# Most K and V loads of a decode block issued by GpSimd as software DMAs instead of by SyncE

## The chip, the cores and the metric

The kernel runs on one core of one Trainium2 chip. Time is device time of one execution in microseconds. The engines are named as in the profile: PE (TensorE, matrix multiplication; PEld are its weight loads), DVE (VectorE), ACT (ScalarE), POOL (GpSimd) and SP (SyncE, which computes nothing and here issues loads). Sixteen DMA engines move the data between the chip's memory and the core's on-chip memory of 128 partitions.

## The reference

One decode step of a transformer block in float32, for two sequences with one new token each. Attention over a cache of 8192 keys, 32 heads of 128, then a residual sum and an MLP (512 to 1792 to 512) with its own layer norms:

```
q = layernorm(x) @ wq                              # 2 x 512 by 512 x 4096
scores = einsum("bhqd,bhkd->bhqk", q, k_cache) * 128 ** -0.5
p = softmax(scores)                                # over 8192 keys
h = x + einsum("bhqk,bhkd->bhqd", p, v_cache) @ wo
y = layernorm(layernorm(h))
out = h + gelu(y @ w1 + b1) @ w2 + b2
```

The caches are 268 MB each, of the 561 MB that the kernel reads. Each number of them is used once.

## The kernel before

**Units and slots.** The work on the caches is cut into 32 units, numbered 0 to 31: unit 2g + b is the pair of heads 2g, 2g + 1 of sequence b. Its K tile and its V tile are 8 MB each: 64 KB in each of 128 partitions (128 rows of 128 numbers). Three slots of this size hold them: K tiles go to slots 0 and 1 in turn, V tiles to slot 2, only the last V tile to slot 1. At the end slot 0 takes wo, and then the weights of the MLP. Text below calls the tiles K0 to K31 and V0 to V31.

**A K tile** is multiplied by q in place by DVE in two chunks (L441), the first of 80 rows and the second of 48. POOL adds the two halves of each row of the first chunk (L445, the halving), DVE sums up the second chunk and then the halved first one (L449), and takes the largest score (L456). Unit 0 has four chunks of 32 and three halvings. After the second unit of a pair, the exponentials (L473, ACT) are made for both.

**A V tile** is used as the moving side of 32 products on PE, in float32 two passes each (L236, or L188 where the code isn't in the loop), two units later: in iteration i the kernel multiplies V of unit i - 2.

**The order of issue.** Each engine works through its own list in the order in which the code is written; waits are set by a helper (class Waits) that follows who wrote and read which part of a tile. One iteration i of the loop writes, in this order: the load of V(i-2) (V0 comes in iteration 1, V1 in iteration 3), the load of K(i+1), the multiplications and the halving of unit i, the products with V(i-2), the sums of unit i. A load waits until the last reader of what its slot held is done: for V that is PE, with the products on the V tile before, for K it is DVE, with the sums of the unit two before it.

**The start.** SP issues wq (8 MB, to slot 2), K0 in two halves and K1 at once; V0 waits for the products with wq.

**The end.** load_wo writes, after the loop, the load of wo by SP into slot 0 and a gather of 64 rows of wog (0.5 MB) by POOL, which is the only software DMA of the kernel. Then follow V30, the projection by wo (project_all), the products with V30, V31 in two parts of 96 and 32 rows of each partition's 128, a memset by POOL for the biases (L590), and the loads of the biases, w1 (L594) and w2 (L598). [...]

**Semaphores.** K and V loads count on one semaphore for each of K and V and each b (waits.own); the other DMAs take 16 in turn for hardware and 16 for software.

Of the kernel before, what the change touches and what calls it, by code (L numbers as in the profile page):

```python
# [16 lines left out]
SHORT = (32, 32, 32, 32)  # L17
NG = 4
TH = 2
FILL = (24, 1, 4, 2, 3)  # L20
SR = 4
LW = 6
# [13 lines left out]
class Waits:  # L36
# [76 lines left out]
    def place(self, eng, op, areas):  # L113
        areas = [(x, w) for x, w in areas if x is not None]
        queue = (eng,)
        if "DMA" in op:
            kind = "soft" if eng == "Pool" else "hard"
            proc = kind, self.lane.get(kind, 0) % self.LANES
            if kind == "hard" and self.own:
                proc = self.own  # L120
            else:
                self.lane[kind] = self.lane.get(kind, 0) + 1
        else:
            proc = queue
        self.sem(proc)
        need = {}
        if proc != queue and self.count[proc]:
            need[proc] = self.count[proc]
        for (name, parts, cols), writes in areas:
            for r in self.mem.get(name, ()):  # L130
                if not (writes or r[4]) or not (r[2] & parts and r[3] & cols):
                    continue
                if r[0] == proc == queue:
                    if eng == "PE" or eng != "Pool" and not r[4]:
                        continue
                need[r[0]] = max(need.get(r[0], 0), r[1])
        clock = self.clock.setdefault(queue, {})
        todo = []
        for p, t in sorted(need.items(), key=lambda x: -self.after[x[0], x[1]][0]):
            if clock.get(p, 0) >= t:  # L140
                continue
            todo.append((p, t))
            for q, u in self.after[p, t][1].items():
                clock[q] = max(clock.get(q, 0), u)
        tick = self.count[proc] + 1
        if op != "Ldweights":
            self.count[proc] = tick
            self.after[proc, tick] = (len(self.after), {**clock, proc: tick})
        for (name, parts, cols), writes in areas:
            held = self.mem.setdefault(name, [])  # L150
            if writes:
                held[:] = [r for r in held if r[2] & ~parts or r[3] & ~cols]
            else:
                held[:] = [r for r in held if r[4] or r[0] != proc or r[2] & ~parts or r[3] & ~cols]
            held.append((proc, tick, parts, cols, writes))
        return proc, todo[::-1]
# [108 lines left out]
def tile_decode_block(nc, waits, x, k, v, wq, wo, wog, w1, bias, w2, out):  # L265
    B, H, SK, DH = k.shape
# [23 lines left out]
    def slot(at):  # L290
        return kv.tile([P, ROW], F32, name="kv", tag="kv", at=at)
# [22 lines left out]
    nc.gpsimd.memset(lt4, 0.0)  # L314
    oall = const.tile([P, H - TH, B], F32, name="oall")
    og = const.tile([P, SR, B], F32, name="og")
# [90 lines left out]
    def load(src, i, parts):  # L407
        g, b = units[i]
        t = slot(i % 2 if src is k or i == NU - 1 else 2)
        rows = src[b, 2 * g:2 * g + 2].rearrange("h (p j) d -> (h p) (j d)", j=NS2)  # L410
        waits.own = ("v" if src is v else "k", b) if len(parts) == 1 else None
        for s0, n in parts:
            nc.sync.dma_start(t[:, s0 * DH:(s0 + n) * DH], rows[:, s0 * DH:(s0 + n) * DH])
        waits.own = None
        return t

# [68 lines left out]
    def values(i, t):  # L485
        g, b = units[i]
        so, nu, w = so2[g == GL], NS2 // 4, 16
        for u in range(nu):
            n = u % NG
            if i == NU - 1 and u == 0:  # L490
                keep_warm(FILL[0])
            pe.matmul(so[32 * n:32 * n + w], ptz[b][:, u, :], t[:, u * 512:(u + 1) * 512],
# [26 lines left out]
    def project_all(wot):  # L519
        so = so2[0]  # L520
        parts = [(oall[:, h, :], wot[:, h, :]) for h in range(GA)]
        parts += [(og[:, r, :], wgt[:, r, :]) for r in range(SR)]
        parts += [(oall[:, h, :], wot[:, h - 2, :]) for h in range(GA + 2, H - TH)]
        n = len(parts)
# [7 lines left out]
    full = [(0, NS2)]  # L532
    assert NS2 == sum(LONG) == sum(SHORT)
    KT, VT = {0: load(k, 0, [(0, NS2 // 2), (NS2 // 2, NS2 // 2)])}, {}
    for i, (g, b) in enumerate(units):
        if i == 1 or i >= 3:
            j = max(i - 2, 0)
            VT[j] = load(v, j, full)
        if i + 1 < NU:
            KT[i + 1] = load(k, i + 1, full)  # L540
# [64 lines left out]
    def cut(parts, n):  # L605
        at[0] += n
        return late[:parts, at[0] - n:at[0]]

    zeros = cut(P, (TH + 1) * 32)
    nc.gpsimd.memset(zeros, 0.0)  # L610
    otz = zeros[:, :TH * 32].rearrange("p (s m) -> p s m", s=TH)
    lane = zeros[:B, TH * 32:]
    nc.gpsimd.tensor_copy(lane[:, 0:B], ident[:B, :B])
# [4 lines left out]

    wl = wot[:, H - 2 - TH:, :]
    wsum = const.tile([P, TH], F32, name="wsum")  # L620
# [20 lines left out]
    def keep_warm(n):  # L641
        for _ in range(n):
            pe.matmul(wp, wb[:, :P], wb, start=True, stop=True)
# [9 lines left out]
    def spread(row):  # L653
        return row.rearrange("d (n j c) -> d n c j", n=NG, c=DC)
# [8 lines left out]
    nc.vector.tensor_copy(b1t, b1p)  # L663
    keep_warm(FILL[1])
    for s in range(TH):
        for n in range(NG):
            pe.matmul(pc[32 * n:32 * n + 32], otz[:, s], spread(wlc[:, s])[:, n], start=False, stop=(s == TH - 1))
    keep_warm(FILL[2])
    cen = cut(P, DC * 32)
# [11 lines left out]
    for s in range(TH):  # L681
        for n in range(NG):
            pe.matmul(po2[32 * n:32 * n + 32], otz[:, s], wl[:, s, n * P:(n + 1) * P], start=False, stop=False)
    keep_warm(FILL[3])
    FH = FN // 2
# [10 lines left out]
    nc.scalar.activation(junk[:, 1:2], std, AF.Gelu_apprx_tanh)  # L696
    keep_warm(FILL[4])

# [67 lines left out]
```

## Time and profile before

| | |
|---|---|
| median of 3 runs | 1303.33 us (1303.16 to 1303.37) |
| profiled execution | 1303.13 us, of which the span of the program is 1301.3 us |
| busy | DVE 973.6 us (75%), PE 385.9 (30%), POOL 364.6 (28%), ACT 49.1 (4%) |
| DMA | 561.13 MB, 431 GB/s over the span; hardware queue 560.48 MB, software queue 0.52 MB |
| chain that ended last | 57% DMA, 37% DVE |

The chain is followed back from the last instruction to what released each step; a wait for a load counts from the load's issue, so that part of a load's time in it is time in the queue behind other loads. Share of 16 engines, in the table of queues, is the time that the packets of a queue took, of what 16 engines have in the span or in the stretch asked for; it can pass 100% in a short stretch, since packets are counted where they start. One packet is one piece of contiguous memory: 64 KB for a K or V tile's partition. Time to landing is from the start of the issuing instruction until the load's semaphore is full.

### The profile page before, as it was taken

What the parts mean: (1) busy time and instruction counts of PE and PEld (TensorE: products, weight loads), DVE (VectorE), ACT (ScalarE), POOL (GpSimd) and SP (SyncE); (2) the same over time, 40 slices, a digit from 0 to 9 for tenths busy, and PEclk for the clock granted to TensorE, in tenths of its full rate; (3) what the DMA queues carried; (4) which work ended last, traced back from release to release, by engine and by line L of the source; (5) the groups of instructions that cost most, each with busy time, mean ns of one, the idle gap of its engine ahead of it and who ended that gap; (6) DMA issues with size and microseconds to landing.
All of it is one profiled execution on the core that took longest, in us unless ns stands there. A gap on an engine that the chain in (4) does not pass through costs nothing.

```text
span 1301.3 us, 6275 instructions
## 1 busy us (share of the span) xinstructions
PE 385.9 (30%) x2756; PEld 118.2 (9%) x2756; DVE 973.6 (75%) x284; ACT 49.1 (4%) x156; POOL 364.6 (28%) x64
## 2 busy tenths in 40 slices
PE   3002322213332122333203232212323212332369
PEld 0000100101010010101001010000101001010113
DVE  1989989777779777779877778877778977777911
ACT  0000000000000000000000000000000000000011
POOL 1433333311333321233321233331133331133300
PEclk9556665566666556666556666556666556666569
DMA  9999999999999999999999999999999999999998
GB/s 403 435 451 420 447 421 445 425 429 439 423 447 423 445 422 447 423 437 433 425 443 425 443 423 447 421 441 429 433 437 423 445 423 447 421 445 425 438 422 373
DMA packets 10821, 561.13 MB, mean 431 GB/s; under 512 B 1398, under 2 KB 1398, under 8 KB 1660
## 3 DMA queue, kind: packets, MB, share of 16 engines
q1 hardware_dynamic: 10664, 560.48, 99.6%
q0 software_dynamic: 144, 0.52, 0.1%
q8 instruction: 5, 0.08, 0.0%
q14 instruction: 4, 0.03, 0.0%
q10 hardware_dynamic: 4, 0.00, 0.0%
HBM read 561.53 MB, written 0.00 MB: 432 GB/s over the span
## 4 chain that ended last, share of the span: by engine, by line
DMA 57%; DVE 37%; issue 2%; POOL 2%; PE 1%; SPq 0%; POOLq 0%
DMA kv<-in_k_dram 50%; DVE kv L441 22%; DVE s L449 15%; DMA kv<-in_w_dram 3%; POOL kv L445 2%; DMA wgt<-in_wog_dram,gidx 2%; DMA kv<-in_wq_dram 2%; PE so L188 1%; DVE qs L395 0%; DVE oall L507 0%; PE qps L188 0%; DVE rl L482 0%; PE sm L236 0%; SPq L598 0%; DVE q L385 0%
## 5 line engine op out<-in xcount | busy, mean ns | idle before, releaser
L441 DVE TENSOR_TENSOR kv<-kv,qps 128x10240 f32<-128x10240 f32 (+1 forms) x66 | 554.5, 8423 | 206.3 <-DMA kv<-in_k_dram 205.8
L445 POOL TENSOR_TENSOR kv<-kv 128x5120 f32<-128x5120 f32 (+1 forms) x34 | 356.0, 10470 | 864.8 <-DVE kv L441 864.8
L236 PE MATMUL so<-kv,pt 128*16 128x512 f32 x1920 | 273.6, 734 | 708.4 <-DMA kv<-in_v_dram 708.4
L449 DVE TENSOR_REDUCE s<-kv 128x48 f32<-128x6144 f32 (+1 forms) x66 | 381.5, 5820 | 1.4 <-POOL kv L445 0.3
L236 PEld LDWEIGHTS so<-kv,pt 128*16 128x16 f32 x1920 | 57.6, 113 | 901.1 <-DMA kv<-in_v_dram 712.6
L497 ACT ACTIVATE ss<-so 128x512 f32<-128x512 f32 x16 | 9.6, 597 | 1062.1 <-PE so L236 1047.8
L473 ACT ACTIVATE pt<-s,nb 64x128 f32<-64x128 f32 x64 | 25.5, 399 | 141.8 <-DVE nb L468 140.5
L236 PE MATMUL sm<-ident,mx 128*1 128x128 f32 x30 | 8.8, 293 | 57.3 <-DVE mx L456 57.3
L461 DVE TENSOR_REDUCE gm<-sm 1x4 f32<-1x256 f32 x16 | 6.6, 412 | 25.5 <-PE sm L236 25.0
L236 PE MATMUL sm<-sel,ss 128*128 128x4 f32 x120 | 15.8, 255 | 12.1 <-ACT ss L497 12.1
L236 PE MATMUL sm<-lt,ones 128*128 128x4 f32 x30 | 8.8, 365 | 34.9 <-ACT pt L473 34.9
L188 PE MATMUL qps<-kv,pt 128*16 128x512 f32 x128 | 16.7, 683 | 6.1 <-DMA kv<-in_v_dram 6.1
L236 PEld LDWEIGHTS sm<-sel,ss 128*128 128x128 f32 x120 | 14.5, 191 | 25.9 <-ACT ss L497 25.9
L385 DVE COPY q<-so 128x512 f32<-128x512 f32 x1 | 0.7, 691 | 20.8 <-PE so L188 20.8
L626 DVE TENSOR_SCALAR kv<-kv,wmean 128x512 f32<-128x512 f32 x2 | 1.0, 518 | 20.3 <-PE qps L188 20.3
L507 DVE TENSOR_TENSOR kv<-sm,rl 128x4 f32<-128x4 f32 x1 | 0.2, 163 | 19.3 <-PE sm L188 19.3
L188 PE MATMUL qps<-kv 128*32 128x128 f32 (+2 forms) x178 | 13.3, 296 | 0.6 <-DMA kv<-in_w_dram 0.6
L188 PE MATMUL so<-kv,yT 128*4 128x512 f32 x64 | 9.9, 787 | 11.5 <-DMA kv<-in_wq_dram 11.5
L188 PE MATMUL sm<-ident,mx 128*1 128x128 f32 x2 | 0.7, 371 | 40.2 <-DVE mx L456 40.2
L473 ACT ACTIVATION_READ_ACCUMULATOR pt<-s,nb 64x1 f32 x64 | 11.8, 184 | 0.0
L236 PE MATMUL qps<-qs,pick 4*128 4x128 f32 x60 | 11.1, 307 | 0.0
L236 PEld LDWEIGHTS sm<-lt,ones 128*128 128x128 f32 x30 | 7.5, 311 | 36.2 <-ACT pt L473 36.2
(108 smaller groups left out, 119.9 us busy)
## 6 DMA issues: line engine op xcount, KB each, us to landing
kv<-in_k_dram SPq DMA_DIRECT2D x2, 4096.0 KB, 35.7
kv<-in_wo_dram SPq DMA_DIRECT2D x1, 7680.0 KB, 46.3
kv<-in_v_dram SPq DMA_DIRECT2D x1, 6144.0 KB, 42.1
kv<-in_w_dram SPq DMA_DIRECT2D x1, 3584.0 KB, 34.3
kv<-in_v_dram SPq DMA_DIRECT2D x1, 2048.0 KB, 46.5
kv<-in_w_dram SPq DMA_DIRECT2D x1, 1792.0 KB, 38.2
kv<-in_w_dram SPq DMA_DIRECT2D x1, 1024.0 KB, 40.2
kv<-in_w_dram SPq DMA_DIRECT2D x1, 512.0 KB, 41.0
```

Of the source, the lines that this page charges most:

```text
L188: getattr(self.nc.tensor, what)(*aps, **how)
L236: ins = getattr(pe, what)(*aps, **how)
L385: nc.vector.tensor_copy(q2, so2[0])
L441: nc.vector.tensor_tensor(kc, kc, QP[g][:, b, None, :].to_broadcast([P, chunks(i)[c], DH]), op=ALU.mult)
L445: nc.gpsimd.tensor_tensor(kc[:, :, 0:HP], kc[:, :, 0:HP], kc[:, :, HP:DH], op=ALU.add)
L449: nc.vector.tensor_reduce(S[i][:, a:z], chunk(i, c, t)[:, :, 0:n], axis=AX.X, op=ALU.add)
L461: nc.vector.tensor_reduce(gm, MT.pop(g).rearrange("o b (s p) -> o b s p", s=2), axis=AX.X, op=ALU.max, negate=True)
L473: nc.scalar.activation(ptz[b][q, :, 4 * m:4 * m + 4], s[q], AF.Exp, bias=nb[q, b, e:e + 1], scale=SCALE, accum_out=lt4[q, m:m + 1])
L497: nc.scalar.activation(SS[g], so2[g == GL], AF.Copy)
L507: nc.vector.tensor_tensor(to, *(x.rearrange("p (b s) -> p s b", b=B) for x in (OP.pop(g), RL.pop(g))), op=ALU.mult)
L626: nc.vector.tensor_scalar(wlc[:, s], wl[:, s], wmean[:, s:s + 1], None, op0=ALU.subtract)
```

## The change

The loads that were all issued by SP are split: K2 to K31 and V0 to V30 go to POOL's list, at the same places of the code, as software DMAs. SP keeps wq, K0, K1, V31, wo, the biases, w1 and w2. Software loads count on the four semaphores of K and V, K1 takes one of the 16 for hardware. JOIN, a flag for the form of the software DMA's packets, is False, which is also what the call has without it.

```diff
+JOIN = False
...
-            if kind == "hard" and self.own:
+            if self.own:
                 proc = self.own
...
-        waits.own = ("v" if src is v else "k", b) if len(parts) == 1 else None
+        soft = len(parts) == 1 and (src is v or i > 1)
+        queue = nc.gpsimd if soft else nc.sync
+        waits.own = ("v" if src is v else "k", b) if soft else None
         for s0, n in parts:
-            nc.sync.dma_start(t[:, s0 * DH:(s0 + n) * DH], rows[:, s0 * DH:(s0 + n) * DH])
+            queue.dma_start(t[:, s0 * DH:(s0 + n) * DH], rows[:, s0 * DH:(s0 + n) * DH], single_packet=soft and JOIN)
         waits.own = None
```

So the order on POOL becomes: the three halvings of unit 0, V0, K2, the halving of unit 1, K3, the halving of unit 2, V1, K4, the halving of unit 3, V2, K5 and so on, at the end V29, the halving of unit 31, the gather of wog, V30, the memset for the biases.

## The prediction, made before the changed kernel was run

> **What bounds the kernel now.** I read the page's span and queues first, then busy time and DMA share by stretch, then three stretches of the timeline.
>
> ```profile
> span 1301.3 us, 6275 instructions
> ...
> q1 hardware_dynamic: 10664, 560.48, 99.6%
> ```
>
> ```profile
> 600.00:1190.00 590.00, 168.44 (x1131) 50.45 (x1135) 460.08 (x117) 20.47 (x72) 173.00 (x16) 0.61 1.00 433
> ```
>
> The hardware queue keeps all 16 DMA engines occupied for 99.6% of the span; in the middle the share is 1.00 at 433 GB/s, while DVE works 460 of 590 us and POOL 173. So nothing but the DMA engines sets the pace there, and a change in who issues counts only where the engines run dry or where the order of arrival changes. One period of the timeline:
>
> ```profile
> 575.78 0.33 SPq L413 DMA_DIRECT2D kv<-in_v_dram  x1
> ...
> 576.54 0.33 SPq L413 DMA_DIRECT2D kv<-in_k_dram  x1
> ...
> 585.38 17.29 DVE L441 TENSOR_TENSOR kv<-kv,qps 128x10240 f32<-128x10240 f32 x2 [8.55 <-DMA kv<-in_k_dram]
> ...
> 596.29 11.05 POOL L445 TENSOR_TENSOR kv<-kv 128x5120 f32<-128x5120 f32 x1 [27.67 <-DVE kv L441]
> ...
> 624.08 10.82 DVE L441 TENSOR_TENSOR kv<-kv,qps 128x10240 f32<-128x10240 f32 x1 [6.55 <-DMA kv<-in_k_dram]
> ```
>
> Two K tiles arrive 624.08 - 585.38 = 38.70 us apart, with one V between them: 19.35 us per 8 MB load, 2.42 us for each of the eight 64 KB rows that an engine moves. When V is issued (575.78) the K load before it is still arriving until 585.38: a load has 9.6 us of cover.
>
> **What a software issue costs.** The kernel has one, the gather of wog:
>
> ```profile
> 1215.84 11.04 POOL L445 TENSOR_TENSOR kv<-kv 128x5120 f32<-128x5120 f32 x1 [27.66 <-DVE kv L441]
> ...
> 1227.06 1.24 POOL L420 DMA_INDIRECT wgt<-in_wog_dram,gidx  x1 [0.18 <-issue]
> ```
>
> The DMA queues from 1227 to 1231.3, from 1231 to 1233, and from 1237 to 1253, and the gather's time to landing:
>
> ```profile
> q1 hardware_dynamic: 31, 1.90, 102.4%
> ```
> ```profile
> q0 software_dynamic: 9, 0.03, 4.1%
> ```
> ```profile
> q1 hardware_dynamic: 121, 6.80, 98.3%
> q0 software_dynamic: 111, 0.44, 6.8%
> ...
> wgt<-in_wog_dram,gidx POOLq DMA_INDIRECT x1, 25.3
> ```
>
> Three things. The gather began only when POOL's halving before it was done (1215.84 + 11.04 = 1226.88): POOL issues in order. It held POOL 1.24 us, and its first packet came after 1231.3, 4.3 us from the issue. And its 0.52 MB, 1.2 us of transfer at 433 GB/s, took 25.3 us: nine pieces on each engine, and before each a whole 64 KB hardware piece (9 x 2.42 = 21.8, plus the 4.3, is 26.1). So the software queue and the hardware queue are served in turn, piece by piece. The pair used 98.3 + 6.8%: taking turns loses nothing.
>
> A hardware issue, with the DMA queues from 1.7 to 2.5 us (there is no packet before 1.7):
>
> ```profile
> 0.74 0.39 SPq L303 DMA_DIRECT2D kv<-in_wq_dram  x1
> ```
> ```profile
> DMA packets 14, 0.92 MB, mean 1147 GB/s; under 512 B 0, under 2 KB 0, under 8 KB 0
> ```
>
> That is 1.0 us from issue to packet. A plain software load is not in this trace. It cannot start sooner than the 1.0, and has no list of indices to read as the gather has, nor (where the engines are dry) another piece to wait for: between 1.0 and 4.3 I take 3.0 us, somewhat nearer the software row.
>
> [...]
>
> **Part 1, the steady state.** 31 V loads and 30 K loads leave SP and take 1.24 us each on POOL. POOL is idle for 27.67 us before the halving at 596.29, and V is issued at 575.78, K at 576.54, so both issues end by about 578.3. The start-up of 3.0 us lies inside the 9.6 us of cover; even 4.3 + 1.24 does. What waits behind an issue is the next halving, due 18 us later. I take 0 (bounds: nothing gained, because a piece at 2.42 us has no row that beats it; up to 3.0 us a load if each waited for the one before, a rival below). Without the cover each load would cost its 3.0 us.
>
> **Part 2, the start.** Here order on POOL decides.
>
> ```profile
> 32.70 0.33 SPq L413 DMA_DIRECT2D kv<-in_v_dram  x1
> ...
> 49.95 4.52 POOL L445 TENSOR_TENSOR kv<-kv 128x2048 f32<-128x2048 f32 x1 [2.25 <-DVE kv L441]
> ...
> 63.16 17.27 DVE L441 TENSOR_TENSOR kv<-kv,qps 128x10240 f32<-128x10240 f32 x2
> ...
> 92.44 0.28 DVE L456 TENSOR_REDUCE mx<-s 128x1 f32<-128x128 f32 x1
> ...
> 105.81 0.33 SPq L413 DMA_DIRECT2D kv<-in_v_dram  x1
> ...
> 110.99 11.03 POOL L445 TENSOR_TENSOR kv<-kv 128x5120 f32<-128x5120 f32 x1 [25.91 <-DVE kv L441]
> ```
>
> V0 stands behind the three halvings of unit 0 and goes out at 54.47 instead of 32.70. K1 is still arriving then; one or two of its pieces let a V0 piece pass, so it lands up to 2.4 to 4.8 us later. In program order V1 stands behind K3 and the halving of unit 2, so it cannot go out before 110.99 + 11.03 = 122.02 instead of 105.81. Time to landing of K1 (issued near 2.2), of K3 (issued at unit 1's end, 92.44) and of V1:
>
> ```profile
> kv<-in_k_dram SPq DMA_DIRECT2D x1, 59.2
> ```
> ```profile
> kv<-in_k_dram SPq DMA_DIRECT2D x1, 28.4
> ```
> ```profile
> kv<-in_v_dram SPq DMA_DIRECT2D x1, 34.4
> ```
>
> K1 landed at 61.4, so it now lands at 63.8 to 66.2 against 63.16 when DVE takes it: unit 1 slips 0.6 to 3, and K3's issue with it, while K2 fills the engines until about 101.4 (K3's landing, 92.44 + 28.4 = 120.8, less 19.35). Cost 0. After K3 nothing else is queued: from 120.8 the engines are dry until 122.02 + 3.0. V1 lands at 125.0 + 19.35 + 0.5 = 144.8 instead of 140.2: **+4.6 us**, for good, because the rest is DMA-bound. With 1.0 or 4.3 us of start-up it is 2.6 or 5.9.
>
> **Part 3, the end.** The wo load (SP, waiting only for DVE) stood behind V29 in one queue. Now V29 is in the software queue and wo alone in the other. All times on the clock of before:
>
> ```profile
> 1194.47 0.33 SPq L413 DMA_DIRECT2D kv<-in_v_dram  x1
> 1196.11 0.33 SPq L419 DMA_DIRECT2D kv<-in_wo_dram  x1
> ...
> 1204.93 17.29 DVE L441 TENSOR_TENSOR kv<-kv,qps 128x10240 f32<-128x10240 f32 x2 [8.53 <-DMA kv<-in_k_dram]
> ...
> 1224.30 9.84 PE L236 MATMUL so<-kv,pt 128*16 128x512 f32 x64 [27.58 <-DMA kv<-in_v_dram]
> ...
> 1234.23 0.29 DVE L456 TENSOR_REDUCE mx<-s 128x1 f32<-128x128 f32 x1
> 1234.29 1.28 SPq L413 DMA_DIRECT2D kv<-in_v_dram  x3
> ...
> 1262.21 9.66 PE L188 MATMUL qps<-kv,pt 128*16 128x512 f32 x64 [6.06 <-DMA kv<-in_v_dram]
> ...
> 1297.01 1.08 PE L188 MATMUL qps<-kv 128*32 128x128 f32 x32 [0.43 <-DMA kv<-in_w_dram]
> 1298.26 1.07 PE L188 MATMUL qps<-kv 128*32 128x128 f32 x24 [0.17 <-DMA kv<-in_w_dram]
> ```
> ```profile
> kv<-in_wo_dram SPq DMA_DIRECT2D x1, 7680.0 KB, 46.3
> ```
>
> - wo's pieces (60 KB, 2.27 us) enter at 1197.1. K31 has 1204.93 - 1197.1 = 7.8 us left, three pieces; with a wo piece to each it lands 6.8 us later, at 1211.7.
> - V29: eight pieces beside the five left of wo, 8 x 2.42 + 5 x 2.27 = 30.7: lands at 1242.4, where wo landed before (1196.11 + 46.3), instead of 1224.3.
> - The matmuls on V29 (9.84) end at 1252.3, and V30, which needs their buffer, goes out then: 18 us later than 1234.29.
> - DVE ends unit 31 at 1234.23 + 6.8 = 1241.0, so the last V, now alone on SP, goes out before V30 and starts at 1242. V30 starts at 1255.3, with 6.2 us of the last V and the gather's 1.2 us to share with: it lands near 1255.3 + 19.4 + 6.8 = 1281.5 instead of 1262.2: **+19.3 us**.
> - From V30's first matmul to the end of the span PE has an in-order chain of 1301.3 - 1262.21 = 39.1 us: V30, fillers, the last V, the MLP. w1 and w2 were waited for 0.43 + 0.17 = 0.6 us; now they are there: -0.6.
>
> SP is emptied of the loads and gains nothing; the memset of the biases on POOL moves behind V30's issue (1253.5), still about 28 us ahead of V30's landing.
>
> **Sum.** 1301.3 + 4.6 + 19.3 - 0.6 = 1324.6 us of span. The profiled execution took 1303.13 us, 1.83 more than its span, and the median is 0.2 above it: 1326.6, say **1326.5 us**. With the bounds of the start-up, and V30 between 1279 (little shared) and 1284.5 (w1's 28 KB pieces in its last turns as well): 1322 to 1331.
>
> **Rivals.**
>
> *The software queue sends a load as one long packet.* If an engine finishes all eight pieces before it turns to wo, V29 waits for one or two wo pieces only and lands at about 1226.5; V30 goes out at 1236.5, waits for the gather and two pieces of the last V and lands at 1266: +3.8, in all 1303.3 + 4.6 + 3.8 = 1311.7 us. [...] The gather, one piece a turn over 25.3 us, speaks against it for its own pieces; loads of 64 KB rows are not shown. 14%.
>
> *Each software load starts with a bubble, or its pieces are slower.* Every 0.1 us a load is 6 us: 0.25 us gives 1342, and a full 3.0 us, if a load only started after the one before, 1509. The 9.6 us of cover and the 105.1% of the mixed window speak against; that no software loads stand back to back anywhere speaks for it. 13%.
>
> *Software pieces are faster* (the other side). There are 61 x 8 = 488 pieces an engine: the change breaks even when a piece takes 2.42 - 23.2 / 488 = 2.37 us, and at 2.35 it ends at 1326.5 - 34.2 = 1292. Place: every K and V load. No row has a piece above 27.1 GB/s an engine (433 / 16). 8%.
>
> *The change doesn't take hold:* POOL issues V1 past the halving, and the wo load is held back by something I don't see: within 2 us of 1303. 5%.
>
> **Chances.** Forecast 60%, the rest as given. A measurement of this kernel tells 0.2%, 2.6 us, from no change. Faster 0.08, same 0.05, slower 0.87. The range 1307 to 1345 takes in the forecast, the long packets and the smaller bubbles, and leaves out the two cases on the other side and the large bubbles.
>
> **What would show it.** In the new profile: V1 issued by POOL at about 122 with the DMA share falling between 121 and 125; the period still 38.7 us; V29's matmuls starting about 18 us later against wo's issue; the last V landing about when V30 does; PE waiting for V30 for some 12 us. Wrong if the period moves (a bubble or a faster piece), or if V29 lands well before wo (long packets).

## The result, and the profile after

| | before | after |
|---|---|---|
| median of 3 runs | 1303.33 us | 1325.21 us (1324.66 to 1326.39) |
| profiled execution, its span | 1303.13, 1301.3 us | 1324.66, 1323.2 us |

The ratio is 1.017, 95% interval 1.0147 to 1.0193: slower by 21.9 us. The prediction was 1326.5 us, in a range of 1307 to 1345.

The page of the changed kernel: span, the two large queues (packets, MB, share of 16 engines), and the software loads as POOL's instructions (busy, mean ns of one, idle before).

```profile
span 1323.2 us, 6275 instructions
...
q0 software_dynamic: 8928, 512.23, 89.5%
q1 hardware_dynamic: 1880, 48.77, 8.6%
...
L416 POOL DMA_DIRECT2D kv<-in_v_dram x31 | 17.7, 570 | 213.4 <-PE so L237 213.4
...
L416 POOL DMA_DIRECT2D kv<-in_k_dram x30 | 16.1, 538 | 35.6 <-DVE s L452 30.3
```

The change does what it says: 31 V and 30 K loads, 512 MB, now come through the software queue, and each takes POOL 0.54 to 0.57 us. Together the queues fill 98.1% of a longer span.

The middle of the run, as a stretch and as one period of the timeline:

```profile
600.00:1200.00 600.00, 174.86 (x1167) 51.60 (x1167) 470.36 (x119) 20.47 (x72) 193.26 (x47) 0.61 1.00 433
```
```profile
581.33 0.56 POOL L416 DMA_DIRECT2D kv<-in_v_dram  x1 [7.46 <-PE so L237]
...
582.10 0.54 POOL L416 DMA_DIRECT2D kv<-in_k_dram  x1 [0.21 <-DVE mx L459]
...
590.64 17.29 DVE L444 TENSOR_TENSOR kv<-kv,qps 128x10240 f32<-128x10240 f32 x2 [8.54 <-DMA kv<-in_k_dram]
...
601.55 11.04 POOL L448 TENSOR_TENSOR kv<-kv 128x5120 f32<-128x5120 f32 x1 [18.91 <-DVE kv L444]
...
629.34 10.82 DVE L444 TENSOR_TENSOR kv<-kv,qps 128x10240 f32<-128x10240 f32 x1 [6.71 <-DMA kv<-in_k_dram]
```

The DMA share is 1.00 at 433 GB/s as before, and two K tiles are 629.34 - 590.64 = 38.70 us apart, as before to the hundredth. Nothing is lost here. But each K tile arrives 5.26 us later than in the kernel before (585.38, 624.08), by an amount that stays.

Where those 5.26 us arise, at the start:

```profile
53.59 0.79 POOL L416 DMA_DIRECT2D kv<-in_v_dram  x1
...
66.44 17.28 DVE L444 TENSOR_TENSOR kv<-kv,qps 128x10240 f32<-128x10240 f32 x2 [4.03 <-DMA kv<-in_k_dram]
...
111.22 11.02 POOL L448 TENSOR_TENSOR kv<-kv 128x5120 f32<-128x5120 f32 x1 [14.65 <-DVE rl L485]
...
122.19 0.56 POOL L416 DMA_DIRECT2D kv<-in_v_dram  x1
...
144.43 9.52 PE L237 MATMUL so<-kv,pt 128*16 128x512 f32 x64 [13.84 <-DMA kv<-in_v_dram]
```

The stretch from 119 to 127 us, first of the kernel before, then of the changed one (the last two columns are DMA share and GB/s), and the DMA answers of the changed kernel for 121 to 123.4, with V1's time to landing, for 118.1 to 123.4 (packets, MB, share) and for 123.4 to 124:

```profile
119.00:127.00 8.00, 0.00 (x0) 0.00 (x0) 8.00 (x2) 0.00 (x0) 3.02 (x1) 0.50 0.90 386
```
```profile
119.00:127.00 8.00, 0.00 (x0) 0.00 (x0) 8.00 (x2) 0.00 (x0) 3.75 (x2) 0.50 0.66 247
```
```profile
DMA packets 0, 0.00 MB, mean 0 GB/s; under 512 B 0, under 2 KB 0, under 8 KB 0
...
kv<-in_v_dram POOLq DMA_DIRECT2D x1, 22.2
```
```profile
q0 software_dynamic: 16, 0.00, 0.2%
```
```profile
q0 software_dynamic: 15, 0.98, 494.2%
```

V1 leaves POOL right behind the halving (111.22 + 11.02). From 118.1 to 123.4 no piece of a load starts: the 16 software packets there carry no data to speak of, and from 121 on there is none at all. Then 15 pieces of V1 begin within 0.6 us, and they take 4.942 x 16 x 0.6 / 15 = 3.16 us each instead of 2.42. V1's products begin at 144.43, 4.17 us later than in the kernel before:

```profile
140.26 9.15 PE L236 MATMUL so<-kv,pt 128*16 128x512 f32 x64 [9.88 <-DMA kv<-in_v_dram]
```

The end:

```profile
1199.89 0.56 POOL L416 DMA_DIRECT2D kv<-in_v_dram  x1 [6.71 <-PE so L237]
1201.10 0.33 SPq L422 DMA_DIRECT2D kv<-in_wo_dram  x1
...
1216.73 17.29 DVE L444 TENSOR_TENSOR kv<-kv,qps 128x10240 f32<-128x10240 f32 x2 [15.34 <-DMA kv<-in_k_dram]
...
1246.03 0.90 SPq L416 DMA_DIRECT2D kv<-in_v_dram  x2
...
1247.46 9.26 PE L237 MATMUL so<-kv,pt 128*16 128x512 f32 x64 [45.74 <-DMA kv<-in_v_dram]
...
1257.13 0.59 POOL L416 DMA_DIRECT2D kv<-in_v_dram  x1 [17.23 <-PE so L237]
...
1286.58 8.47 PE L189 MATMUL qps<-kv,pt 128*16 128x512 f32 x64 [11.26 <-DMA kv<-in_v_dram]
...
1321.44 0.32 DVE L714 STREAM_TRANSPOSE kv<-qps 128x128 f32<-128x128 f32 x1 [2.40 <-PE qps L189]
```

The wo load's time to landing, and the DMA queues from 1204.5 to 1236.9, that is, from wo's first piece to its last, beside the end of K31 and then V29:

```profile
kv<-in_wo_dram SPq DMA_DIRECT2D x1, 7680.0 KB, 40.9
```
```profile
DMA packets 240, 14.16 MB, mean 437 GB/s; under 512 B 16, under 2 KB 16, under 8 KB 16
...
q1 hardware_dynamic: 128, 7.86, 56.1%
q0 software_dynamic: 112, 6.29, 44.9%
```

On 16 engines that is 8 pieces of wo and 7 software packets each, just as many as fit between 8: the two queues are served one packet each in turn. Within that time, in each 4.9 us from 1214.3 to 1233.9, 18 to 20 software and 16 hardware packets start. Of the 7, one is a packet of under 512 B at the end of K31, and the count comes out only if that one takes a turn too. wo lands at 1242.0, V29, which was issued before it, at 1247. V31 goes out on SP at 1246, V30 on POOL at 1257. PE waits 11.3 us for V30, whose products begin at 1286.58 instead of 1262.21.

### The profile page after: what moved, and what is told of

The parts are those of the page before. It is cut to its first block, busy times and chain, and to the rows that moved or that the text cites. A ratio compares the mean times of both kernels' runs of the same rounds, so it can differ in the third digit from the quotient of the medians.

```text
span 1323.2 us, 6275 instructions
## 1 busy us (share of the span) xinstructions
PE 385.8 (29%) x2756; PEld 118.6 (9%) x2756; DVE 973.7 (74%) x284; ACT 49.1 (4%) x156; POOL 397.9 (30%) x125
## 3 DMA queue, kind: packets, MB, share of 16 engines
q0 software_dynamic: 8928, 512.23, 89.5%
q1 hardware_dynamic: 1880, 48.77, 8.6%
## 4 chain that ended last, share of the span: by engine, by line
DMA 71%; PE 24%; DVE 3%; POOL 1%; issue 1%
DMA kv<-in_v_dram 67%; PE so L237 20%; DMA kv<-in_k_dram 3%; PE qps L189 2%; DVE kv L444 2%; DMA kv<-in_wq_dram 2%; POOL kv L448 1%; DVE s L452 1%; PE so L189 1%; PE sm L189 0%; PE rowacc L189 0%; DVE q L386 0%; DVE kv L677 0%; DVE kv L673 0%; DVE kv L714 0%
## 5 line engine op out<-in xcount | busy, mean ns | idle before, releaser
L452 DVE TENSOR_REDUCE s<-kv 128x48 f32<-128x6144 f32 (+1 forms) x66 | 381.5, 5821 | 1.4 <-POOL kv L448 0.3
L416 POOL DMA_DIRECT2D kv<-in_v_dram x31 | 17.7, 570 | 213.4 <-PE so L237 213.4
L464 DVE TENSOR_REDUCE gm<-sm 1x4 f32<-1x256 f32 x16 | 6.6, 412 | 38.1 <-PE sm L237 37.7
L416 POOL DMA_DIRECT2D kv<-in_k_dram x30 | 16.1, 538 | 35.6 <-DVE s L452 30.3
L189 PE MATMUL qps<-kv,pt 128*16 128x512 f32 x128 | 15.5, 641 | 11.3 <-DMA kv<-in_v_dram 11.3
L510 DVE TENSOR_TENSOR kv<-sm,rl 128x4 f32<-128x4 f32 x1 | 0.2, 164 | 18.1 <-PE sm L189 18.1
## 6 DMA issues: line engine op xcount, KB each, us to landing
kv<-in_wo_dram SPq DMA_DIRECT2D x1, 7680.0 KB, 40.9
kv<-in_v_dram SPq DMA_DIRECT2D x1, 6144.0 KB, 19.3
kv<-in_v_dram SPq DMA_DIRECT2D x1, 2048.0 KB, 40.9
```

The source lines that it names most:

```text
L189: getattr(self.nc.tensor, what)(*aps, **how)
L416: queue.dma_start(t[:, s0 * DH:(s0 + n) * DH], rows[:, s0 * DH:(s0 + n) * DH], single_packet=soft and JOIN)
L452: nc.vector.tensor_reduce(S[i][:, a:z], chunk(i, c, t)[:, :, 0:n], axis=AX.X, op=ALU.add)
L464: nc.vector.tensor_reduce(gm, MT.pop(g).rearrange("o b (s p) -> o b s p", s=2), axis=AX.X, op=ALU.max, negate=True)
L510: nc.vector.tensor_tensor(to, *(x.rearrange("p (b s) -> p s b", b=B) for x in (OP.pop(g), RL.pop(g))), op=ALU.mult)
```

## The experiments

The theory: the software loads as such cost nothing, and the change costs by order alone, at two places. At the start V1 stands behind a halving on POOL; at the end loads that stood in one line are served in turn from two queues. The rival: some cost belongs to each of the 61 software loads (22/61 = 0.36 us each).

**V1 ahead of the halving.** In iteration 2 the halving is written behind the load of V1.

```diff
-        if i == 1 or i >= 3:
+        if i == 1 or i > 3:
...
-            if c < nch - 1:
+            if c < nch - 1 and i != 2:
                 halve(i, c, kt)
...
             values(i - 2, VT.pop(i - 2))
+            if i == 2:
+                VT[1] = load(v, 1, full)
+                halve(i, 0, kt)
```

> The changed kernel, with the halving of unit 2 written behind the load of V1 on POOL instead of ahead of it; nothing else moves. Theory (order on POOL makes the dry stretch at 121 us): V1 goes out when the products with V0 end, near 110 us instead of 122.2, while K3 is still arriving; the DMA share no longer falls between 120 and 125, and every later K tile lands where it did before the change (K landing for DVE near 624.1 instead of 629.3), so the time falls by 4.2 to 5.3 us, to about 1320 us. Rival (a software load by itself is slower or starts late, and the 5.3 us are the sum of that): the K tiles stay at 629, the time at 1325.

Measured: 1320.0 us, ratio to before 1.0126 (1.0108 to 1.0144), 5.2 us less than the changed kernel. Its timeline and its stretch from 119 to 127:

```profile
110.51 0.54 POOL L416 DMA_DIRECT2D kv<-in_v_dram  x1 [14.15 <-PE so L237]
111.06 11.04 POOL L448 TENSOR_TENSOR kv<-kv 128x5120 f32<-128x5120 f32 x1
...
624.04 10.82 DVE L444 TENSOR_TENSOR kv<-kv,qps 128x10240 f32<-128x10240 f32 x1 [7.03 <-DMA kv<-in_k_dram]
```
```profile
119.00:127.00 8.00, 0.00 (x0) 0.00 (x0) 8.00 (x2) 0.00 (x0) 3.10 (x1) 0.50 0.90 386
```

V1 goes out 11.7 us earlier, the share in the stretch is 0.90 again, and the K tile that came at 629.34 comes at 624.04, as before the change (624.08). The whole 5.26 us of the middle belonged to one load's place in POOL's list.

**wo in line with V29.** wo is issued by POOL, behind V29's load and ahead of unit 31's halving; the gather stays where it was.

```diff
-        nc.sync.dma_start(t, wo)
+        nc.gpsimd.dma_start(t, wo)
...
         if i + 1 < NU:
             KT[i + 1] = load(k, i + 1, full)
+        else:
+            wot = load_wo()
```

> The changed kernel, with the wo load issued by POOL right behind V29's (ahead of the halving of unit 31) instead of by SP; V31 and the weights of the MLP stay on SP. Both theories agree that V29's products start about 18 us earlier against unit 30 (near 1229.5 instead of 1247.5). Theory A (V30 is late because V29 and with it the issue of V30 were late, the prediction's chain): V30 goes out near 1239.5 and its products start 15 to 19 us earlier than in the changed kernel, time about 1308. Theory B (what costs is that V30 shares the DMA engines with V31 from another queue, and work ahead of both is the same): wo and the gather now stand ahead of V30 in the software queue while V31 takes turns with them from 1240 on, so V30 lands where it did or up to 3 us later, time 1325 to 1329.

Measured: 1328.07 us (four runs, 1327.32 to 1335.56), 1.0208 (1.0173 to 1.0244): no faster than the changed kernel, 2.9 us above its median. Its timeline:

```profile
1229.30 9.82 PE L237 MATMUL so<-kv,pt 128*16 128x512 f32 x64 [27.58 <-DMA kv<-in_v_dram]
...
1239.21 0.80 SPq L416 DMA_DIRECT2D kv<-in_v_dram  x2
...
1239.53 0.58 POOL L416 DMA_DIRECT2D kv<-in_v_dram  x1 [6.44 <-PE so L237]
...
1289.59 8.69 PE L189 MATMUL qps<-kv,pt 128*16 128x512 f32 x64 [18.91 <-DMA kv<-in_v_dram]
```

V29 is on time (1229.30 is 1224.30 plus the start's 5), V30 goes out 17.6 us earlier than in the changed kernel, and its products begin 3 us later still. V31 goes out on the other queue at the same moment, first beside wo, then beside V30: DVE's sum over wo, which waits for the load, begins at 1251.06, with V31 in line (the next run) at 1247.99. V31's turns were not counted here. That was theory B: to have V29 on time is not enough. The run does not show how much of V30's time here goes to V31's turns and how much to wo, which now stands ahead of it.

**The end in line.** As the last, and V31, w1 and w2 by POOL too, in the order of before.

```diff
-        queue = nc.gpsimd if soft else nc.sync
+        queue = nc.gpsimd if soft or i == NU - 1 else nc.sync
...
-    nc.sync.dma_start(w1t, w1v)
+    nc.gpsimd.dma_start(w1t, w1v)
...
-        nc.sync.dma_start(w2t[:, t:t + n, :], w2v[:, t:t + n, :])
+        nc.gpsimd.dma_start(w2t[:, t:t + n, :], w2v[:, t:t + n, :])
```

> As the run with wo in line, and V31, w1 and w2 are issued by POOL too, V31 behind V30: from V29 on everything large is in the one software queue, in the order of before the change. Both theories of turns between two queues: V30's products start near 1262.2 + 5.3 = 1267.5, the end is that of before plus the start's 5.3 us: about 1308 to 1310. Rival (software loads cost by themselves at the end, for example the slower start of each): stays above 1318.

Measured: 1308.35 us, 1.0039 (1.0024 to 1.0054), 16.9 us less than the changed kernel. V30's products, in its timeline:

```profile
1268.44 9.20 PE L189 MATMUL qps<-kv,pt 128*16 128x512 f32 x64 [9.44 <-DMA kv<-in_v_dram]
```

That is 1262.21 and the start's shift, 1267.5, to within a microsecond, with more software loads than in the changed kernel.

**Both places in order.** The edits of the first and the third run together.

> The halving of unit 2 behind V1's load, and everything large from V29 on in the software queue. Theory (the change costs only by order: 5 us at the start, 17 at the end, and nothing for each load): 1303 to 1305 us, the same as before the change within 0.2%. Rival (some part of the 22 us belongs to the 61 software loads themselves): what is left above 1303 is that part.

Measured: 1302.88 us, 0.9997 (0.9987 to 1.0007). Nothing is left of the 22 us, though now 536 of the 561 MB come by the software queue. The rival of a cost for each load falls; so do the prediction's rivals of a bubble and of faster pieces. The kernel does not beat the one before.

**Only w1 and w2 back on SP**, from the kernel with both places in order.

```diff
-    nc.gpsimd.dma_start(w1t, w1v)
+    nc.sync.dma_start(w1t, w1v)
...
-        nc.gpsimd.dma_start(w2t[:, t:t + n, :], w2v[:, t:t + n, :])
+        nc.sync.dma_start(w2t[:, t:t + n, :], w2v[:, t:t + n, :])
```

> The kernel with both places put in order, but w1 and w2 issued by SP again: V30 and V31 stay in line in the software queue, and the weights, which nothing needs until the products with V31 are done, come in the other queue from 1254 us on. Theory (turns): V30's products start some 3 to 4 us later (near 1266), V31's first part lands near 1294 instead of 1277, and the last product with it ends 17 us late: 1312 to 1321 us. Rival (only V29, V30 and V31 out of line with each other matter): 1303.

Measured: 1314.77 us, 1.009 (1.0073 to 1.0107). V30's products, and V31's in two lots:

```profile
1265.58 8.73 PE L189 MATMUL qps<-kv,pt 128*16 128x512 f32 x64 [12.97 <-DMA kv<-in_v_dram]
...
1287.05 8.22 PE L189 MATMUL qps<-kv,pt 128*16 128x512 f32 x48 [7.45 <-DMA kv<-in_v_dram]
1295.57 1.91 PE L189 MATMUL qps<-kv,pt 128*16 128x512 f32 x16 [0.30 <-DMA kv<-in_v_dram]
```

V30's products begin 3.1 us later than in the kernel with both places in order (1262.44), V31's 9.4 us later (1277.62), the whole takes 12 us more (1302.88), and only the queue of w1 and w2 differs. So weights that PE does not want before V31's products are done hold up loads that it waits for. The packets were not counted here; that the weights do it by turns is the theory's account. The products with V31's first part began at 1287, where 1294 was expected for its landing. How the 17 us at the end divide between wo, V31 and the weights when each alone is left on SP was not run, except for the weights.

**Only V, and only K, as software loads.** The first keeps all K loads on SP, the second all V loads.

```diff
-        soft = len(parts) == 1 and (src is v or i > 1)
+        soft = len(parts) == 1 and src is v
```
```diff
-        soft = len(parts) == 1 and (src is v or i > 1)
+        soft = len(parts) == 1 and src is k and i > 1
...
-        waits.own = ("v" if src is v else "k", b) if soft else None
+        waits.own = ("v" if src is v else "k", b) if len(parts) == 1 and (soft or src is v) else None
```

> Only V's loads but the last go to POOL; all K loads stay on SP. That halves the number of software loads (31 instead of 61) but puts K and V in two queues through the whole run. Theory (queues are served in turn, so a K tile now shares the engines with the V tile issued at the same time, lands up to 10 us later in each period, DVE ends later and the engines run dry): about 1410 us, 8% slower than before, the period of a pair of loads near 42 instead of 38.7 us. Rival (a software load costs 22/61 = 0.36 us by itself): about 1314 us.

> The other half: only K's loads from the third on go to POOL, all V loads stay on SP. Theory (in turn): as with V alone, about 1410 us. Rival (0.36 us for each of 30 software loads): about 1314 us.

Measured: 1457.23 us, 1.1182 (1.1159 to 1.1204), and 1430.41 us, 1.0976 (1.0954 to 1.0998). Half as many software loads, and six to seven times the loss. The stretch from 600 to 1200, first with V, then with K as software loads, and three groups of the page of the first:

```profile
600.00:1200.00 600.00, 150.51 (x1022) 44.77 (x1022) 419.62 (x105) 17.92 (x63) 162.38 (x28) 0.61 0.89 380
```
```profile
600.00:1200.00 600.00, 150.91 (x998) 44.16 (x1002) 419.63 (x105) 17.32 (x62) 162.35 (x28) 0.60 0.89 383
```
```profile
L444 DVE TENSOR_TENSOR kv<-kv,qps 128x10240 f32<-128x10240 f32 (+1 forms) x66 | 554.2, 8419 | 7.6 <-DMA kv<-in_k_dram 7.1
L237 PE MATMUL so<-kv,pt 128*16 128x512 f32 x1920 | 273.0, 732 | 877.3 <-DMA kv<-in_v_dram 877.3
...
L464 DVE TENSOR_REDUCE gm<-sm 1x4 f32<-1x256 f32 x16 | 6.6, 412 | 379.2 <-PE sm L237 378.7
```

The engines' share falls to 0.89, so two queues cost time as the theory said, but not as it described it. K is not late (DVE waits 7.1 us for it, 206 before); V is. The softmax of each pair (L464) waits for PE, which has the products with a late V in front of it, 379 us in all, and meanwhile DVE frees no K slot. With K as software loads the page shows the same: DVE waits 15.5 us for K, and 344 us at L464. Nor does DVE wait for POOL's halvings: its sums (L452) stand idle for 1.4 us in all in both runs. The size was off by 47 and 20 us against 1410, and why the two differ was not settled.

**The packet flag, JOIN True**, on the changed kernel. The theory takes the flag to make one packet of a software load's eight pieces on an engine, so that the prediction's rival of long packets would come about; that was the author's guess, and no run shows it.

```diff
-JOIN = False
+JOIN = True
```

> [...] Theory (turns between queues go by packets): V29's products start only 2 to 5 us later against wo's issue than before the change, and V30's lateness shrinks from 19 to about 4 us. But at the start K1 on the hardware queue has one or two pieces left when V0's packet begins, and each must wait for a whole software load: with one piece left K1 lands near 80.5 instead of 65.9, unit 1 is late, K3 goes out after the engines are dry, about 8 us more at the start, in all about 1318; with two left K1 lands after K2 (about 100) and the time is about 1344. Rival (the flag does not touch the turns): V29 late as in the changed kernel, time 1325.

Measured: 1325.8 us, 1.0173 (1.0156 to 1.019), the changed kernel's time; V29's products begin at 1247.50 (1247.46 without the flag), and wo lands after 40.9 us as there. Over the span its queues count 8928 software and 1880 hardware packets, the very numbers of the changed kernel. So the flag does not touch the turns of loads in 64 KB rows, and what else it does no run here shows. It could not make the rival of long packets; that rival falls by the changed kernel's own 128 against 112.

**One queue from K1 on, with the flag.** Both places in order, JOIN True, and `i > 0` in place of `i > 1`, so that K1 is POOL's too.

> The kernel with both places put in order, K1 issued by POOL as well, and JOIN True for the whole K and V tiles: now next to nothing shares the engines with a joined packet. Theory (the pace is that of the DMA engines, and a 64 KB piece costs 2.42 us where the slope from 32 KB to 64 KB pieces, 1.207 us for 32 KB more, would give 2.41): joining can save at most 0.01 us a piece, about 5 us in all: 1298 to 1304. [...]

Measured: 1316.04 us, 1.0098 (1.0081 to 1.0115), outside the theory's 1298 to 1304. K1's issue in its timeline, and the landing of K0's halves:

```profile
6.21 0.79 POOL L416 DMA_DIRECT2D kv<-in_k_dram  x1
```
```profile
kv<-in_k_dram SPq DMA_DIRECT2D x2, 4096.0 KB, 55.1
```

K1 no longer stands behind K0 on SP; it goes out at 6.2 us and shares the engines with wq, which lands after 33.9 instead of 21.9 us, and K0, which lands after 55.1 instead of 35.7. To tell this from the flag, K1 went back to SP with the flag kept:

> The kernel with both places put in order and JOIN True, but K1 back on SP: it separates the two edits of the run that had K1 on POOL and JOIN together (1316.0 us). Theory (the flag changes nothing, as in the changed kernel, and the 12.8 us belonged to K1, which went out at the start and took turns with wq and K0): 1303 us, the same as before. Rival (joined packets cost, and only where nothing else shares the engines): near 1316.

Measured: 1302.8 us, 0.9997 (0.9987 to 1.0007). The flag does nothing here either, and the 13 us were K1's place.

## Why the prediction was right, by its own steps

- **The steady state** (cost 0): right. Period 38.70 us, share 1.00, both issues inside the cover; an issue takes POOL 0.56 us, not the gather's 1.24. In order, the kernel of software loads takes 1302.88 us.
- **The start** (+4.6): right in place, and near in size: 4.17 us by V1's products, 5.26 by the later K tiles, 5.2 by the run that undoes it. V1 went out at 122.19 (predicted 122.02). Inside the term two sizes were wrong. From issue to packet it took 1.26 us and not 3.0, and the load itself took 22.2 - 1.26 = 20.9 us and not 19.85 (19.35 and an estimate of 0.5), for its first pieces took 3.16 us. The engines also began to run dry earlier than the forecast 120.8: no piece starts from 118.1 on, so that the last of K3's, at 2.42 us each, was through by 120.5 and most were through before it. These errors cancel in part, so that 4.6 came so near is partly luck. Nor is V1's 1.26 us a constant: V0 took 4.5 us (last section).
- **K1** was predicted to land at 63.8 to 66.2; DVE took it at 66.44, and no gap followed.
- **The end** (+19.3): right in its numbers. Beyond the start's 5.26, K31 was 6.5 us late (6.8 predicted), V29 17.9 (18.1), V30's issue 17.6 (18), V30's products 19.1. V30's own time, 29.45 us from its issue to its products, was forecast as 3.0 + 19.4 + 6.8 = 29.2, again with errors that cancel. The 6.8 was not the sum of its parts (6.2 for V31 and 1.2 for the gather make 7.4), and the gather had landed by 1248.2 (1238.84 + 9.4), before V30 went out. The first packet came 5.0 us after the issue and not 3.0, which leaves 29.45 - 5.0 - 19.35 = 5.1 us for turns with others. The chain behind V30 was 2.5 us shorter, not 0.6: V30's products took 8.47 instead of 9.66 us, and the chain from V31's products to the end was 1.3 us shorter, 0.6 of it the predicted waits for w1 and w2. The rest the prediction did not have. The fillers in that chain are 24 products without use between V30's and V31's; the granted clock was 1.00 in them (before, 1271.8 to 1277.1), and no run leaves them out.
- **The sum**: 1301.3 + 5.26 + 19.1 - 2.5 = 1323.2, the span.
- **What the prediction's reason left out**: "V29 late, so V30 goes out 18 us later, so it lands 19 us later" took place in the changed kernel, but it is not enough as a reason. In the run with wo in line V29 is on time, V30 goes out 17.6 us earlier, and it lands no earlier. What the two kernels share is V31 on the other queue: it goes out no later than V30, and nearly all of its 8 MB, worth 19.35 us at the pace of the middle, is through when V30 has landed. With V31 and the weights in V30's queue the 17 us are gone. The prediction had V31 ahead of and beside V30 in its sum, but put the whole price down to the late issue, which was one way to the same turns.
- **Rivals**: long packets fell by the turns, 128 packets against 112, in pieces of 60 and 64 KB, with 18 to 20 software and 16 hardware packets in each 4.9 us from 1214.3 to 1233.9. The bubble and the faster piece fell by the period and by the run with both places in order, and the change took hold.

## What to carry to other kernels

Where the DMA engines set the pace, as here with a share of 1.00, the queue a load is issued on decides its place among the others: the two queues of this kernel were served in turn (128 packets against 112), so a load that nobody waits for took about every second piece from one that an engine waited for. Move loads to another queue together with everything that must stay behind them, and look at what stands ahead of them on the new issuer's list: here one halving of 11 us cost 5 us, and wo, V31 and the weights of the MLP, left behind on the other queue, cost 17. With everything in line, which kind of DMA moved these 8 MB loads made no difference (a ratio of 0.9997).

## What was not expected of the hardware

The time from issue to first packet was not one number. V1, with the engines dry, had its first packet 1.26 us after the issue. V0, issued at 53.59 beside K1, had none before 58, and V30, issued at 1257.13 beside V31, none before 1262 (first packets at 58.1 and 1262.2). The queues from 53.5 to 58 and from 1257 to 1262 have packets of the hardware queue alone:

```profile
q1 hardware_dynamic: 23, 1.51, 77.3%
```
```profile
q1 hardware_dynamic: 35, 1.72, 79.4%
```

It is not a matter of software loads alone: wo, issued by SP at 1201.10, had its first piece at 1204.6, 3.5 us later, where wq took 1.0 us at the start of the program. The three late ones have other loads under way, V1 and wq have none, and the gather's 4.3 us in the prediction may be of the same kind. What a load waits for in that time was not tested.

In the kernel with both places in order, POOL's last w2 load was held:

```profile
1253.45 1.56 POOL L608 DMA_DIRECT2D kv<-in_w_dram  x3
1262.44 9.96 PE L189 MATMUL qps<-kv,pt 128*16 128x512 f32 x64 [8.39 <-DMA kv<-in_v_dram]
1262.70 0.54 POOL L608 DMA_DIRECT2D kv<-in_w_dram  x1 [7.69 <-issue]
```

It was the eighth software load under way, behind V30, V31 in two parts, w1 and three of w2, and it went out 0.26 us after V30's products began, that is, once V30 had landed. The program gives it nothing to wait for. The run with both in order, JOIN True and K1 on SP shows the same hold, of 7.71 us. What held it was not tested. It cost no time here: the run took 1302.88 us.
